# Raw weights' buffers for the last input forms, and an earlier request for u, in a one-core attention, gate and mixer kernel

## The chip, the cores and the metric

The kernel runs on one NeuronCore of a Trainium2 chip, as one launch. The metric is the time of an execution on the device in microseconds, the median of several runs. Before the change it is 718.12 us (three runs, 717.54 to 718.13).

## What is computed

Three stages over `batch = 4`, `seq = 448`, `d_model = 768` (12 heads of 64), all in float32 accuracy. The change lies in the second half of the third one, the channel mixer `u + relu(u @ w_ch1) @ w_ch2`, with `d_ch = 1536`.

```python
def _attn_ref(q, k, v):
    scores = scale * np.matmul(q, k.transpose(0, 1, 3, 2)) - np.log(S)
    attn = 1.0 / (1.0 + np.exp(-scores))
    return np.matmul(attn, v).astype(np.float32)

def _moe_ref(x, w_val, conv_w, w_out):
    for k in range(K):
        gate_pre += conv_w[k][None, None, :] * xp[:, k:k + S, :]
    gate = 1.0 / (1.0 + np.exp(-gate_pre))
    val = x @ w_val
    return (gate * val @ w_out).astype(np.float32)

def _moe2_ref(x, w_tok1, w_tok2, w_ch1, w_ch2):
    xt = x.transpose(0, 2, 1)
    h = np.maximum(xt @ w_tok1, 0.0) @ w_tok2
    u = x + h.transpose(0, 2, 1)
    h2 = np.maximum(u @ w_ch1, 0.0) @ w_ch2
    return (u + h2).astype(np.float32)
```

## The kernel before

Matrix products take each float32 operand as two parts, a high one in the format `F32R` and the rest, and add three matmuls (high by high, low by high, high by low). The first 384 us hold attention, the gated layer and the token mixer; `u` is left in a DRAM scratch, `uscr`, channels by positions. The change touches only what follows.

The channel mixer goes over the 1792 positions in four tiles of 512, 512, 384 and 384 (`TILES`), and over the 1536 inner channels in 12 steps of 128 (`fc`). In the first two tiles step `fc` is a `ch1` (18 matmuls into one of the two PSUM buffers `psh`, then a `split` with relu by ScalarE and VectorE into `r`), followed by the `ch2` of the step before (18 matmuls into six accumulators `pso`). At the last step each of the six accumulators gets the input added: `u` is loaded again into a buffer of the tag `gate` (`ur`, by `u_load`), VectorE adds the accumulator to it (L778), and SP sends it to `out` (L780).

The third and fourth tile share their first matrix product by Strassen's and Winograd's scheme: seven products of half size in place of eight. For it, `sums(i)` forms sums of the weights beside the second tile and stores them through SP into the scratch `fscr`; their operands `sum_s` and `sum_h` take both buffers of the tag `raw` of the pool `rp["a"]`, which held the raw weights before. `turned_load(k)` loads four blocks of `u` for the third and fourth tile (`ub`), and `turned(k)` makes the seven forms of the input of group `k` from them, with two more buffers, `t1` and `t2` (`ut`), for differences; k goes from 0 to 2. A form is a high part by ScalarE (L926) and a low part by VectorE (L930), with differences by VectorE (L934) between them.

After the second tile, `seven(i)` runs six times: seven calls of `product`, each nine matmuls into one of two PSUM buffers `psm`, emptied by ScalarE (L983) or by an add on VectorE (L987) into buffers `um`. Behind every `seven` but the first stand two `ch2` of the third tile; the fourth tile's `ch2` come last. The weights of a product, a form `wf`, are loaded by POOL's queue (`form_load`, L962) into six buffers, and every product asks for the form that is six ahead.

The tag `gate` has six buffers of 2 KB a partition, given out in turn, and `ub`, `ut`, `ur` and `um` all use them. A buffer is given again once its last reader, a DMA too, is through.

From the second tile's second step on the order is written out by hand (`tc.manual_schedule`): each engine and each DMA queue takes its instructions in program order and waits only for semaphores. The table `beside` says behind which `ch1` of the second tile which helper stands: `turned_load(2)` behind the tenth (`fc` 9) and `turned(2)` behind the last (`fc` 11). Behind the last `ch1` also stand six `form_load` and `ur_load`, which asks for all six `ur`:

```python
if fn is ch1 and fc == KF - 1:
    for _ in range(KD):
        form_load()
    ur_load(t)
```

For the first tile nothing of this is written out: there the last `ch2` asks for each `ur` itself, in a part of the program that a scheduler orders, which puts these loads some eleven us ahead of their use.

Of the kernel before, what the change touches and what calls it, by code (L numbers as in the profile page):

```python
# [8 lines left out]
F32 = mybir.dt.float32  # L9
# [25 lines left out]
def tile_kernel(ctx, tc, qT, kT, v, w_val, conv_w, w_out, w_tok1, w_tok2, w_ch1, w_ch2, out):  # L35
# [11 lines left out]
    P = 128  # L47
# [12 lines left out]
    KH = KD // 2  # L60
# [5 lines left out]
    W = max(TILES)  # L66
# [6 lines left out]
    NJ = TILES[-1]  # L73
# [3 lines left out]
    def f(ap):  # L77
        return ap.bitcast(F32)
# [95 lines left out]
    both = tc.alloc_tile_pool(name="both", bufs=1, side="left")  # L174
# [466 lines left out]
    rp = {}  # L641
# [75 lines left out]
        return ops  # L717


    def u_load(t, j, name):  # L720
        u = both.tile([P, W], F32, tag="gate", bufs=6, name=name)
        lo, hi = sum(TILES[:t]), sum(TILES[: t + 1])
        for b in range(lo // S, (hi - 1) // S + 1):
            c0, c1 = max(lo, b * S), min(hi, (b + 1) * S)
            nc.sync.dma_start(u[:, c0 - lo : c1 - lo], uscr[b, j, :, c0 - b * S : c1 - b * S])
        return u[:, : hi - lo]

    def prep_load(t, j):
        us_t[t, j] = u_load(t, j, "u")
# [31 lines left out]
    def ur_load(t):  # L761
        for j in range(KD):
            ur[t, j] = u_load(t, j, "ur")

    def ch2(t, fc):
        n_t = TILES[t]
        r = r_t.pop((t, fc))
        for j in range(KD):
            if fc == 0:
                acc[j] = pso.tile([P, 512], F32, tag=f"o{j}", name="pso")  # L770
            for n, (a, c) in enumerate(((0, 0), (1, 0), (0, 1))):
                nc.tensor.matmul(  # L772
                    acc[j][:, :n_t], wch[fc][1][a][:, j * P : (j + 1) * P], r[c],
                    start=fc == 0 and n == 0, stop=fc == KF - 1 and n == 2,
                )
            if fc == KF - 1:
                u = ur.pop((t, j)) if (t, j) in ur else u_load(t, j, "ur")
                nc.vector.tensor_tensor(out=u, in0=acc[j][:, :n_t], in1=u, op=ALU.add)  # L778
                lo = sum(TILES[:t])
                nc.sync.dma_start(out[j * P : (j + 1) * P, lo : lo + n_t], u)  # L780

    with tc.manual_schedule():
# [23 lines left out]
        for b in range(B):  # L806
            val, outs, after = dense_steps(b, tok[3] if b else ([], []))
            if b:
                early = val[0] + tok[0] + val[1] + tok[1]
                rest = sum(val[2:], []) + tok[2]  # L810
                if b + 1 < B:
                    ops = first.pop(0)
                    n = len(PRE)
# [59 lines left out]
    def form_room():  # L873
        if not room:
            fc = form_room.at
            form_room.at += 1
            if 0 < fc < CHAN_LATE:
                get = w_tile if fc < CHAN_HELD else wo_tile
                room.extend(get().rearrange("p (c m) -> p c m", c=2) for _ in range(2))
            else:  # L880
                t = rp["p" if fc else "a"].tile([P, 2, 2, HALF], F32R, tag=f"wch{fc}_0", bufs=1, name="bf")
                room.extend(t[:, n] for n in range(2))
        return room.pop(0)
# [30 lines left out]
    ub = {}  # L914

    def turned_load(k):
        ub[k] = [u_load(t, k + h, "ub") for h in (0, KH) for t in (2, 3)]

    def turned(k):
        b11, b12, b21, b22 = ub.pop(k)  # L920
        t1, t2 = [both.tile([P, W], F32, tag="gate", bufs=6, name="ut")[:, :NJ] for _ in range(2)]
        to = {}

        def high(name, src):
            to[name] = src, form_room()
            nc.scalar.activation(out=to[name][1][:, 0], in_=src, func=AF.Copy)  # L926

        def low(name):
            src, x = to.pop(name)
            nc.vector.tensor_tensor(out=x[:, 1], in0=src, in1=f(x[:, 0]), op=ALU.subtract)  # L930
            bform[name, k] = x

        def sub(o, x, y):
            nc.vector.tensor_tensor(out=o, in0=x, in1=y, op=ALU.subtract)  # L934

        high("b11", b11)
        sub(t1, b12, b11)
        high("t1", t1)
        low("b11")
        sub(t2, b22, t1)  # L940
        high("t2", t2)
        low("t1")
        high("b22", b22)
        low("t2")
        sub(b12, b22, b12)
        high("t3", b12)
        low("b22")
        high("b21", b21)
        low("t3")
        sub(t1, b21, t2)  # L950
        high("t4", t1)
        low("b21")
        low("t4")
# [4 lines left out]
    def form_load():  # L958
        if queue:
            i, name = queue.pop(0)  # L960
            t = both.tile([P, 2, HALF], F32R, tag="xs", bufs=KD, name="wf")
            nc.gpsimd.dma_start(t, fscr[i, spot[name]])  # L962
            held_f[i, name] = t
# [13 lines left out]
    def seven(i):  # L977
        def spare():
            return both.tile([P, W], F32, tag="gate", bufs=6, name="um")[:, :NJ]

        def out(ps):
            t = spare()
            nc.scalar.activation(out=t, in_=ps, func=AF.Copy)  # L983
            return t

        def add(o, x, y):
            nc.vector.tensor_tensor(out=o, in0=x, in1=y, op=ALU.add)  # L987

        m1 = out(product(i, "a11", "b11"))
        u = spare()  # L990
        add(u, product(i, "s2", "t2"), m1)
        m5 = out(product(i, "s1", "t1"))
        v = spare()
        add(v, u, m5)
        add(v, product(i, "s4", "b22"), v)
        nc.sync.dma_start(rscr[2 * i], v)
        add(u, product(i, "s3", "t3"), u)
        add(m5, u, m5)
        nc.sync.dma_start(rscr[2 * i + 1], m5)
        r = rp["a"].tile([P, 2, 2, NJ], F32R, tag="raw", bufs=2, name="rr")  # L1000
        add(m1, product(i, "a12", "b21"), m1)
        split(r[:, 0, 0], r[:, 0, 1], m1, relu=True)
        add(u, product(i, "a22", "t4"), u)
        split(r[:, 1, 0], r[:, 1, 1], u, relu=True)
        for n in range(2):
            r_t[2, 2 * i + n] = [r[:, n, c] for c in range(2)]
# [3 lines left out]
    def r_load(fc):  # L1010
        if fc < KF:
            back[fc] = both.tile([P, W], F32, tag="gate", bufs=6, name="rl")[:, :NJ]
            nc.sync.dma_start(back[fc], rscr[fc])

    def r_split(fc):
        if fc < KF:
            r = rp["p"].tile([P, 2, W], F32R, tag="r", bufs=2, name="r")
            r = [r[:, c, :NJ] for c in range(2)]
            split(*r, back.pop(fc), relu=True)
            r_t[3, fc] = r  # L1020
# [11 lines left out]
    for fn, t, fc in order[:cut]:  # L1032
# [5 lines left out]
        elif fn is ch2 or t or fc >= EARLY:  # L1038
            fn(t, fc)
    with tc.manual_schedule():  # L1040
        beside = {1: (sums, 0), 2: (sums, 1), 3: (sums, 2), 4: (turned_load, 0, sums, 3), 5: (turned, 0)}
        beside |= {6: (sums, 4), 7: (turned_load, 1, sums, 5), 8: (turned, 1), 9: (turned_load, 2), 11: (turned, 2)}
        for fn, t, fc in order[cut:]:
            fn(t, fc)
            if fn is ch1:
                todo = beside.get(fc, ())
                for n in range(0, len(todo), 2):
                    todo[n](todo[n + 1])
            if fn is ch1 and fc == KF - 1:
                for _ in range(KD):  # L1050
                    form_load()
                ur_load(t)
        for i in range(KF // 2):
            seven(i)
            if i:
                for fc in (2 * i - 2, 2 * i - 1):
                    ch2(2, fc)
        for fc in range(2):
            r_load(fc)
            r_split(fc)  # L1060
        ur_load(2)
        ch2(2, KF - 2)
        ch2(2, KF - 1)
        r_load(2)
        for fc in range(KF):
            r_load(fc + 3)
            if fc == KF - 2:
                ur_load(3)
            ch2(3, fc)
            r_split(fc + 2)  # L1070
# [42 lines left out]
```

## Time and profile before

| | before |
|---|---|
| median of 3 runs | 718.12 us |
| profiled execution | 716.71 us |
| its span, first to last instruction | 714.9 us |
| mean granted clock of TensorE | 0.995 of full |
| TensorE busy | 702.4 us, 98% |
| VectorE / ScalarE / GpSimd busy | 480.8 / 305.3 / 90.5 us |
| moved by DMA | 128.16 MB, 179 GB/s in the mean |

Times in the rows are microseconds from the start of the span. L778 is line 778 of the kernel before. PE is TensorE's matmuls, PEld its weight loads, DVE is VectorE, ACT ScalarE, POOL GpSimd; SPq is SyncE's queue of DMA issues. A row of a timeline merges neighbouring instructions of one kind (x18: eighteen of them) and gives in brackets how long the engine was idle before and what ended that.

### The profile page before, as it was taken

What the parts mean: (1) busy time and instruction counts of PE and PEld (TensorE: products, weight loads), DVE (VectorE), ACT (ScalarE), POOL (GpSimd) and SP (SyncE); (2) the same over time, 40 slices, a digit from 0 to 9 for tenths busy, and PEclk for the clock granted to TensorE, in tenths of its full rate; (3) what the DMA queues carried; (4) which work ended last, traced back from release to release, by engine and by line L of the source; (5) the groups of instructions that cost most, each with busy time, mean ns of one, the idle gap of its engine ahead of it and who ended that gap; (6) DMA issues with size and microseconds to landing.
All of it is one profiled execution on the core that took longest, in us unless ns stands there. A gap on an engine that the chain in (4) does not pass through costs nothing.

```text
span 714.9 us, 11033 instructions
## 1 busy us (share of the span) xinstructions
PE 702.4 (98%) x4210; PEld 576.1 (81%) x4210; DVE 480.8 (67%) x789; ACT 305.3 (43%) x454; POOL 90.5 (13%) x128
## 2 busy tenths in 40 slices
PE   8999999999999999999999999999999699999998
PEld 3444444699999999999988888888888599999997
DVE  1799775479899998976778999557771533232322
ACT  5899888347336435624733444312331211111110
POOL 0000110003213213301340000000000122220000
PEclk9999999999999999999999999999999999999999
DMA  9747998504346324236994555339882986664533
GB/s 296 250 136 235 276 289 271 168 26 99 64 164 178 69 96 131 67 127 188 224 350 146 169 166 177 89 119 340 291 280 62 298 243 182 193 182 131 184 102 110
DMA packets 102212, 128.16 MB, mean 179 GB/s; under 512 B 35072, under 2 KB 89104, under 8 KB 102160
## 3 DMA queue, kind: packets, MB, share of 16 engines
q1 hardware_dynamic: 90672, 90.40, 41.6%
q0 software_dynamic: 11056, 36.61, 15.9%
q8 instruction: 33, 0.54, 0.3%
q10 hardware_dynamic: 432, 0.46, 0.2%
q14 instruction: 19, 0.16, 0.1%
HBM read 83.98 MB, written 37.16 MB: 169 GB/s over the span
## 4 chain that ended last, share of the span: by engine, by line
PE 92%; DMA 3%; DVE 2%; ACT 1%; issue 1%; SPq 0%; DVEq 0%; ACTq 0%
PE psd L359 24%; PE pso L772 23%; PE psh L745 12%; PE psm L970 9%; PE psy L296 8%; PE pss L281 8%; PE pst L423 4%; PE pst L436 4%; DMA raw<-w_ch 1%; DMA out<-ur 1%; DMA k<-kT 1%; DMA ur<-uscr 1%; ACT ga L283 0%; DVE dec_a L135 0%; DVE x2T L440 0%
## 5 line engine op out<-in xcount | busy, mean ns | idle before, releaser
L283 ACT ACTIVATE ga<-pss,bias_s 128x896 f32<-128x896 f32 x84 | 83.5, 1004 | 19.7 <-PE pss L281 19.1
L359 PE MATMUL psd<-gv,wo 128*128 128x448 f32 x432 | 88.0, 362 | 0.0
L359 PE MATMUL psd<-xs,w 128*128 128x448 f32 x432 | 87.7, 362 | 0.0
L359 PEld LDWEIGHTS psd<-xs,w 128*128 128x128 f32 x432 | 80.8, 187 | 6.0 <-issue 0.7
L359 PEld LDWEIGHTS psd<-gv,wo 128*128 128x128 f32 x432 | 81.0, 187 | 5.4
L281 PE MATMUL pss<-q,k 64*64 64x448 f32 x672 | 78.9, 540 | 1.2 <-DMA k<-kT 0.7
L296 PE MATMUL psy<-ga,v 64*64 64x448 f32 x672 | 77.6, 536 | 0.0
L329 DVE SCALAR_TENSOR_TENSOR gate<-xb,cw,gate 128x448 f32<-128x448 f32 x96 | 72.2, 752 | 2.6
L281 PEld LDWEIGHTS pss<-q,k 64*64 64x64 f32 x672 | 26.3, 134 | 39.7 <-issue 29.3
L296 PEld LDWEIGHTS psy<-ga,v 64*64 64x64 f32 x672 | 25.7, 133 | 37.4 <-issue 35.9
L962 POOL DMA_DIRECT2D wf<-fscr x42 | 22.2, 528 | 245.9 <-PE psh L745 167.1
L135 DVE SCALAR_TENSOR_TENSOR dec_a<-raw,dec_a 128x768 int32<-128x768 int32 (+2 forms) x38 | 33.4, 880 | 20.8 <-ACT dec_a L123 20.8
L123 ACT ACTIVATE dec_a<-dec_a,exp_b 128x768 int32<-128x768 int32 (+3 forms) x39 | 33.0, 858 | 32.6 <-DVE dec_a L120 32.6
L987 DVE TENSOR_TENSOR um<-psm,um 128x384 f32<-128x384 f32 x30 | 16.7, 556 | 43.8 <-PE psm L970 43.0
L394 POOL COPY pl<-st 128x1024 uint16<-128x1024 uint16 x21 | 32.1, 1529 | 102.2 <-ACT gate L340 50.8
L970 PE MATMUL psm<-bf,wf 128*128 128x384 f32 x162 | 36.8, 342 | 6.1 <-ACT um L983 6.1
L370 ACT ACTIVATE gv<-gate 128x448 fp32r<-128x448 f32 x24 | 13.9, 578 | 56.5 <-DVE gate L368 56.5
L94 DVE SCALAR_TENSOR_TENSOR r<-psh,r 128x512 fp32r<-128x512 f32 x22 | 15.0, 688 | 30.1 <-ACT r L92 30.1
L772 PE MATMUL pso<-r,wo 128*128 128x512 f32 (+1 forms) x162 | 35.0, 371 | 0.0
L970 PEld LDWEIGHTS psm<-bf,wf 128*128 128x128 f32 x162 | 29.5, 193 | 6.5 <-ACT um L983 6.4
L772 PEld LDWEIGHTS pso<-r,wo 128*128 128x128 f32 x162 | 29.7, 188 | 4.2
L772 PE MATMUL pso<-r,w 128*128 128x512 f32 (+1 forms) x144 | 30.7, 368 | 0.0
(200 smaller groups left out, 1270.7 us busy)
## 6 DMA issues: line engine op xcount, KB each, us to landing
raw<-w_ch SPq DMA_DIRECT2D x24, 768.0 KB, 4.4
wf<-fscr POOLq DMA_DIRECT2D x42, 384.0 KB, 4.4
v<-v SPq DMA_DIRECT2D x24, 224.0 KB, 6.4
uscr<-x2T POOLq DMA_DIRECT2D x24, 224.0 KB, 2.4
q<-qT SPq DMA_DIRECT2D x23, 224.0 KB, 4.5
k<-kT SPq DMA_DIRECT2D x22, 224.0 KB, 4.7
raw<-w_out POOLq DMA_DIRECT2D x6, 768.0 KB, 8.5
fscr<-sum_h SPq DMA_DIRECT2D x6, 768.0 KB, 3.4
```

The source lines that it names most:

```text
L123: nc.scalar.activation(out=t["a"], in_=t["a"], func=AF.Relu, scale=8.0, bias=exp_b)
L135: nc.vector.scalar_tensor_tensor(out=t["a"], in0=hi, scalar=-0x80000000, in1=t["a"], op0=ALU.bitwise_and, op1=ALU.bitwise_or)
L281: nc.tensor.matmul(ps[cols, j, :S], k[rows, keys], q[rows], start=True, stop=True)
L283: nc.scalar.activation(out=a, in_=ps[:, :, :S], func=AF.Sigmoid, bias=bias_s, scale=QK_SCALE)
L296: nc.tensor.matmul(y_t[i + h][cols, :S], v_t[i][rows, c, cols], a[rows, j], start=c == 0, stop=c == NB - 1)
L329: nc.vector.scalar_tensor_tensor(out=acc, in0=x[:, t : t + S], scalar=w, in1=acc, op0=ALU.mult, op1=ALU.add)
L359: nc.tensor.matmul(ps[:, :S], w(a, kk), s[:, c, :], start=kk == 0 and n == 0, stop=kk == KD - 1 and n == 2,)
L394: nc.gpsimd.tensor_copy(back.rearrange("p (n h) -> p h n", h=2), st.rearrange("p h c d -> p h (c d)"))
L423: nc.tensor.matmul(ps[:, :HALF], a, x[:, m], start=n == 0, stop=n == len(mm) - 1)
L745: nc.tensor.matmul(ps[:, :n_t], wch[fc][0][a][:, kk * P : (kk + 1) * P], us_t[t, kk][:, c, :], start=kk == 0 and n == 0, stop=kk == KD - 1 ...
L772: nc.tensor.matmul(acc[j][:, :n_t], wch[fc][1][a][:, j * P : (j + 1) * P], r[c], start=fc == 0 and n == 0, stop=fc == KF - 1 and n == 2,)
L970: nc.tensor.matmul(ps, w[:, a, k * P : (k + 1) * P], bform[x, k][:, c], start=k == 0 and n == 0, stop=k == KH - 1 and n == 2,)
```

## The change

`u_load` may be given a place instead of taking a `gate` buffer. For the last group, k = 2, `turned_load` takes both `raw` buffers of `rp["a"]`: the four `ub` go into the first, and `t1` and `t2` into the second, so that this group uses no `gate` buffer. And `ur_load(t)` moves from behind the last `ch1` of the second tile to behind its tenth (`fc` 9), right behind `turned_load(2)`.

```diff
-    def u_load(t, j, name):
-        u = both.tile([P, W], F32, tag="gate", bufs=6, name=name)
+    def u_load(t, j, name, u=None):
+        u = both.tile([P, W], F32, tag="gate", bufs=6, name=name) if u is None else u
...
     def turned_load(k):
-        ub[k] = [u_load(t, k + h, "ub") for h in (0, KH) for t in (2, 3)]
+        at = [None] * 6
+        if k == KH - 1:
+            spare = [rp["a"].tile([P, 4, NJ], F32, tag="raw", bufs=2, name="ub") for _ in range(2)]
+            at = [spare[n // 4][:, n % 4] for n in range(6)]
+        ub[k] = [u_load(t, k + h, "ub", at[2 * n + t - 2]) for n, h in enumerate((0, KH)) for t in (2, 3)], at[4:]
 
     def turned(k):
-        b11, b12, b21, b22 = ub.pop(k)
-        t1, t2 = [both.tile([P, W], F32, tag="gate", bufs=6, name="ut")[:, :NJ] for _ in range(2)]
+        (b11, b12, b21, b22), t = ub.pop(k)
+        if t[0] is None:
+            t = [both.tile([P, W], F32, tag="gate", bufs=6, name="ut")[:, :NJ] for _ in range(2)]
+        t1, t2 = t
...
             if fn is ch1 and fc == KF - 1:
                 for _ in range(KD):
                     form_load()
+            if fn is ch1 and fc == 9:
                 ur_load(t)
```

On no engine does the change move an instruction past another: TensorE's and POOL's rows are the same, and on SP, VectorE and ScalarE the same operations stand in the same order, with other waits. (Line numbers of the kernel after are up to 7 higher.) In the rows below, a semaphore DMAHW0 to DMAHW7 is one of those that SP's DMAs count up in turn; DVE, PE and Activation are the engines' own.

SP's queue, from the loads of `ub` for k = 2 to the first loads of `ur` for the second tile, before:

```order
L912 DMA fscr<-sum_s 128x4x384 [waits DMAHW7_49,DVE_49]
L725 DMA ub<-uscr 128x320 [waits DMAHW0_49,DVE_49]
L725 DMA ub<-uscr 128x64 [waits DMAHW1_49,DMASW4_49]
L725 DMA ub<-uscr 128x384 [waits DMAHW2_49,DVE_49]
L725 DMA ub<-uscr 128x320 [waits DMAHW3_49,DVE_49]
L725 DMA ub<-uscr 128x64 [waits DMAHW4_49,DMASW7_49]
L725 DMA ub<-uscr 128x384 [waits DMAHW5_49,DVE_49]
L725 DMA ur<-uscr 128x384 [waits DMAHW1_49,DMAHW6_49,DMAHW0_49,DVE_49]
L725 DMA ur<-uscr 128x128 [waits DMAHW7_49]
```

and after:

```order
L912 DMA fscr<-sum_s 128x4x384 [waits DMAHW7_49,DVE_49]
L725 DMA ub<-uscr 128x320 [waits DMAHW6_49,DMAHW0_49]
L725 DMA ub<-uscr 128x64 [waits DMAHW1_49,DMASW4_49]
L725 DMA ub<-uscr 128x384 [waits DMAHW2_49]
L725 DMA ub<-uscr 128x320 [waits DMAHW3_49]
L725 DMA ub<-uscr 128x64 [waits DMAHW4_49,DMASW7_49]
L725 DMA ub<-uscr 128x384 [waits DMAHW5_49]
L725 DMA ur<-uscr 128x384 [waits DVE_49]
L725 DMA ur<-uscr 128x128 [waits DMAHW7_49]
```

The loads of `ub` no longer wait for VectorE but for a store of SP (DMAHW6, that of `sum_h`); the first `ur` no longer waits for DMAs, only for VectorE, whose count here is one of `turned(1)`.

ScalarE at the end of `turned(2)`, where the first two evictions of a product (`um`) stand, before:

```order
L926 ACTIVATE bf<-ub 128x384 [waits DMAHW5_49]
L926 ACTIVATE bf<-ub 128x384 [waits DVE_49]
L926 ACTIVATE bf<-ub 128x384 [waits DMAHW4_49,DMAHW3_49]
L926 ACTIVATE bf<-ut 128x384 [waits DMAHW2_49,DVE_49]
L983 ACTIVATE um<-psm 128x384 [waits DMAHW2_49,DMAHW6_49,DVE_49,DMAHW7_49,PE_49,Activation_49]
L983 ACTIVATE um<-psm 128x384 [waits DMAHW3_49,DVE_49,DMAHW4_49,PE_49,Activation_49]
```

and after:

```order
L932 ACTIVATE bf<-ub 128x384 [waits DMAHW5_49]
L932 ACTIVATE bf<-ub 128x384 [waits DVE_49]
L932 ACTIVATE bf<-ub 128x384 [waits DMAHW4_49,DMAHW3_49]
L932 ACTIVATE bf<-ub 128x384 [waits DMAHW2_49,DVE_49]
L989 ACTIVATE um<-psm 128x384 [waits DMAHW6_49,DMAHW2_49,DMAHW7_49,DVE_49,PE_49]
L989 ACTIVATE um<-psm 128x384 [waits DMAHW3_49,DMAHW4_49,DVE_49,PE_49]
```

Nothing moved; `t1` and `t2` are now called `ub`, and the evictions still wait for SP's DMAs, the store of the `ur` whose `gate` buffer they take among them (DMAHW2 for the first, DMAHW4 for the second).

## Rows read from the trace of the kernel before

**Rows 1.** The page: busy us of each engine, share of the span, instructions.

```profile
PE 702.4 (98%) x4210; PEld 576.1 (81%) x4210; DVE 480.8 (67%) x789; ACT 305.3 (43%) x454; POOL 90.5 (13%) x128
```

**Rows 2.** The chain of waits, 540 to 600: start us, us, what.

```profile
557.83 5.04 DMA ur<-uscr
...
565.50 6.25 DMA out<-ur
...
571.99 0.50 ACT um L983
```

**Rows 3.** TensorE's timeline, 526 to 618: start us, us, engine, line, operation.

```profile
563.14 0.69 PE L970 MATMUL psm<-bf,wf 128*128 128x384 f32 x3
...
572.53 1.33 PE L970 MATMUL psm<-bf,wf 128*128 128x384 f32 x3 [6.09 <-ACT um L983]
...
592.72 3.28 PE L772 MATMUL pso<-rr,wch__3250 128*128 128x384 f32 x18
...
598.96 0.68 PE L970 MATMUL psm<-bf,wf 128*128 128x384 f32 x3
...
609.88 6.40 PE L772 MATMUL pso<-rr,w 128*128 128x384 f32 x36
```

**Rows 4.** Stretches: length, each engine's busy us, granted clock, DMA share, GB/s.

```profile
572.50:575.50 3.00, 2.96 (x9) 2.97 (x10) 0.56 (x1) 0.00 (x0) 0.00 (x0) 0.51 0.53 196
575.50:592.70 17.20, 17.20 (x100) 17.20 (x100) 7.91 (x15) 3.06 (x6) 5.81 (x11) 1.00 0.88 244
592.70:714.90 122.20, 118.74 (x686) 118.42 (x684) 33.94 (x63) 14.76 (x29) 12.14 (x23) 1.00 0.50 153
```

**Rows 5.** SP's queue of DMA issues, end of the first and the second tile.

```profile
455.25 5.81 SPq L725 DMA_DIRECT2D ur<-uscr  x12
467.37 3.32 SPq L780 DMA_DIRECT2D out<-ur  x6
...
531.61 0.53 SPq L912 DMA_DIRECT2D fscr<-sum_s  x1
533.32 4.50 SPq L725 DMA_DIRECT2D ub<-uscr  x6
557.46 7.94 SPq L725 DMA_DIRECT2D ur<-uscr  x12
565.50 6.62 SPq L780 DMA_DIRECT2D out<-ur  x6
```

**Rows 6.** VectorE's timeline at the same two places.

```profile
466.66 3.67 DVE L778 TENSOR_TENSOR ur<-pso,ur 128x512 f32<-128x512 f32 x6
...
537.59 0.56 DVE L930 TENSOR_TENSOR wo<-ut,wo 128x384 fp32r<-128x384 f32 x1
...
561.73 0.56 DVE L930 TENSOR_TENSOR bf<-ut,bf 128x384 fp32r<-128x384 f32 x1
562.99 2.10 DVE L778 TENSOR_TENSOR ur<-pso,ur 128x512 f32<-128x512 f32 x3 [0.70 <-DMA ur<-uscr]
```

**Rows 7.** Median us from issue to landing: first tile's first store; `sum_s` of 531.61.

```profile
out<-ur SPq DMA_DIRECT2D x1, 256.0 KB, 2.0
...
fscr<-sum_s SPq DMA_DIRECT2D x1, 768.0 KB, 6.7
```

**Rows 8.** POOL's queue of DMA issues, 526 to 600.

```profile
552.04 1.89 POOL L962 DMA_DIRECT2D wf<-fscr  x3 [167.10 <-PE psh L745]
...
566.75 0.53 POOL L962 DMA_DIRECT2D wf<-fscr  x1 [1.04 <-DMA ur<-uscr]
```

**Rows 9.** Form loads' us to landing: issued 555 to 556, and all of 545 to 600.

```profile
DMA to landing us min/median/max: 5.3/5.5/5.6
...
DMA to landing us min/median/max: 3.1/4.6/8.2
```

**Rows 10.** Two more stretches, columns as in rows 4.

```profile
470.00:472.00 2.00, 2.00 (x10) 1.67 (x9) 0.32 (x1) 0.00 (x0) 0.00 (x0) 1.00 1.05 396
...
563.10:566.30 3.20, 3.20 (x19) 2.99 (x18) 2.47 (x4) 0.00 (x0) 0.53 (x1) 1.00 0.81 231
```

## The prediction

> **What bounds the kernel now.** I read the page's busy times first: TensorE is busy for 702.4 of 714.9 us [rows 1], so only what makes TensorE idle, or slows it, can move the time. Then the chain of waits, to find a stretch that isn't TensorE. Around the end of the second tile (its last `ch2`, then the first two calls of `seven`) it leaves TensorE for a load of `ur`, a store of `ur` to `out` and an eviction on ScalarE, and only then comes the next product [rows 2]. Third, TensorE in order of time: it starts the first product at 563.14, runs two products at full pace, and is then idle for 6.09 us until 572.53 [rows 3]. It has two PSUM buffers for products; the third product needs the first one's, which ScalarE must empty into a buffer of the tag `gate`, and that buffer still holds the first `ur`, on its way to `out`.
>
> The same stretch also runs slowly behind the gap. The granted clock is 0.51 from 572.5 to 575.5 and 1.00 from 575.5 on [rows 4]: the lower of the two levels (1.2 and 2.4 GHz) after an idle stretch, then the upper.
>
> The loss is the stretch against the same work undisturbed. Fourteen products run from 563.14 to 592.72, which is 29.58 us. A later call of `seven`, seven products, runs from 598.96 to 609.88, 10.92 us or 1.56 a product [rows 3]; two calls are 21.84. So 29.58 - 21.84 = 7.74 us are lost. In parts: two products at full pace end at 563.14 + 3.12 = 566.26, and the third starts at 572.53, 6.27 later; the third's nine matmuls fill 572.5 to 575.5 [rows 4], 3.00 us for 1.56, so 1.44 more; the other eleven run at full pace, within 0.03. From 592.7 on TensorE is busy without a pause at full clock until the tail [rows 4], so what is saved here moves everything behind it.
>
> Why the store is late: SP's queue issues the twelve loads of `ur` only from 557.46 to 565.40, and the six stores stand behind them [rows 5]. Before that it issues nothing from 537.8 on, since it waits for VectorE's `turned(2)`, whose operands fill all six `gate` buffers. The first add is through by 563.7 [rows 6], but its store is issued at 565.50 and lands 6.25 us later, with the last loads of `ur` and the form loads moving beside it [rows 2].
>
> **The change, part by part.**
>
> *The last input forms in the raw buffers.* No computation is added: VectorE and ScalarE get the same operations of the same shapes in the same order, so `turned(2)` still ends on VectorE at 561.73 + 0.56 = 562.29 [rows 6]. What is new is what the six loads of `ub` wait for: no longer the `gate` operands of `turned(1)`, but the raw buffers' last stores, `sum_h` and `sum_s` of `sums(5)`. The later was issued at 531.61 [rows 5] and landed 6.7 us later [rows 7], at 538.3. SP stands still for them, and behind them stand only the loads of `ur`, until the outputs. If all six wait for 538.3 and take the 4.50 us of issue that they took before [rows 5], they are issued by 542.8; `turned(2)` wants them at 556. Cost: nothing, under some 13 us of cover, less the landing. The raw buffers are wanted again by `rr` in the first `seven`, some ten us after `turned(2)` is through; also nothing.
>
> *The `ur` loads behind the tenth step.* SP's order doesn't change: `ub`, then `ur`, then `out`. Only the waits do. The `gate` buffers are now free once `turned(1)` has ended (537.59 + 0.56 = 538.15 [rows 6]), so the twelve loads follow `ub` at once: 542.8 + 5.81 (the first tile's twelve [rows 5]) = 548.6, and even at the 6.25 us of this tile's store [rows 2] they are there by 555. Neither SP's queue nor POOL's issues anything in that stretch before [rows 5, 8], so it collides with nothing, and the form loads, from 552 on, lose the `ur` traffic beside them. The adds need `ur` at 562.3; some 7 us are left over.
>
> *What is late next* is the store of the first `ur`. VectorE goes from `turned(2)` to the adds at 562.29. The first tile is the model, since its `ur` is loaded early: six adds in 3.67 us from 466.66, the first store issued at 467.37, 0.71 after the first add began [rows 5, 6]. So the first store is issued at 562.29 + 0.71 = 563.0. How long it takes is not shown for this place; the bounds are 2.0 us (the first tile's first store [rows 7]) and 6.25 (this tile's, behind the `ur` loads [rows 2]). I take 2.0: as in the first tile nothing is queued ahead, since the first six form loads are issued by 556 and the last of them took at most 5.6 us even with `ur` beside them [rows 9]. Then it lands at 565.0, as the first product ends (563.14 + 1.56, and the last matmul's tail); ScalarE's 0.50 us [rows 2] make 565.5; and the third product's buffer is free before the second product ends at 566.26. The margin is 0.7 us: each us of landing over 2.7 costs one.
>
> The next in line is VectorE: its six adds end at 562.29 + 3.67 = 565.96, and the add that empties the second product's buffer (0.56, as its other operations on 128x384) ends at about 567.1, against 567.8 when the third product ends. The second to fourth stores, issued some 0.6 us apart, land by 568; the buffers that they free are wanted at 566.5, 567.9 and 568.5. No stall above half a us; I take none.
>
> The sum: 7.74 us off a profiled execution of 716.71 (span 714.9) is 708.97. That execution was 1.41 below the median of 718.12, so against the median it is 718.12 - 7.74 = **710.4 us**.
>
> *The form loads behind the stores.* The gap gave the DMA a rest that now goes: 1.57 MB of stores (six of 256 KB) meet one form load of 0.39 MB per 1.56 us. The seventh and eighth form load are issued as the first two products end (about 565.2, and 566.75 [rows 8]) and wanted at 572.5 and 574.1, when the seventh and eighth product start. Form loads land in 4.6 us in the median and 8.2 at most [rows 9]. At 8.2 the eighth would come at 574.95, 0.9 late. DMA moved 396 GB/s for the first tile's stores, and 231 in the mixed stretch from 563.1 [rows 10]. From 564 to 567, 2.35 MB of stores and form loads come up. At 396, 1.16 MB are left, 2.9 us of work, and with the 2.0 us of a lone store as latency the eighth lands at 572: in time. At 231 it is 1.66 MB, 7.2 us, and the eighth is some 2 us late; all that the fourteenth product needs (stores, eight form loads, 0.6 MB of `rscr`, 5.3 MB) is there at 587 instead of 583.4, near 4 late. I take the upper rate, because in the slower stretch the loads of `ur` in their short rows and SP's issue held it down, and keep the lower one for the range.
>
> A rule of the Trainium skill speaks against this: "DMA: Bandwidth & Descriptors", section "Specifications", gives some 358 GB/s as the limit of one core's share of HBM. All that is issued in the 21.84 us (six stores, fourteen form loads, four `rscr` stores, 7.86 MB) is 360 GB/s, just over that; by it I estimate 21.96 us for the stretch and 710.5 for the kernel. The trace's 396 GB/s in a stretch of writes to HBM [rows 10] stands above the page's figure already.
>
> **The rivals.**
> - *The first store stays slow.* If form loads get in first and it lands after 4 to 6.25 us, the third product waits 1.3 to 3.55 us; with another 1.44 if the clock falls again, 711.7 to 715.4. Against it: the first tile's 2.0.
> - *Form loads late.* The gap closes, but the eighth to fourteenth form load comes 1 to 4 us late, as worked out above: 711.4 to 714.4.
> - *The change doesn't do what it says.* If SP's queue were still held until `turned(2)`, by a raw buffer say, the loads of `ur` would come as now: 718.1. Against it: what now stands first in SP's order waits for stores that landed by 538.3.
> - *Slower.* The mechanism is the clock: late form loads make repeated pauses, and the clock stays at its lower level for all twelve products behind the second. Each costs 1.44 us more, 17.3 in all, less 7.74: 727.7. It decides from 5.4 slow products on. Against it: at 3.0 us a product the form loads are wanted at half the rate, so DMA catches up; and in the trace one slow product was enough to return to full clock [rows 4].
>
> **How the numbers follow.** Full gain 0.70 (710.4), slow first store 0.12, late form loads 0.12, no effect 0.03, slower 0.03. The range must leave out at most 2 in 10: from 708.9 (the 1.41 by which single executions differ, taken off) to 713.8, which takes in most of both partial cases. A difference of 0.2% (1.4 us) is about what can be told from no change; faster by more than that is 0.70 + 0.12 + 0.12 = 0.94, within it 0.03, slower 0.03.
>
> **What the changed profile would show.** Right: loads of `ur` issued between 538 and 549 on SP; the first store issued at about 563.0 and landing in 2 to 3 us; no idle TensorE behind 566, granted clock 1.00 there, 21.8 us from the first product to the first `ch2` of the third tile; a span of about 707.2; no `ur` in this part of the chain of waits. Wrong: an idle stretch ahead of the third product that ends on ScalarE and a store (first rival), one ahead of the eighth or a later product that ends on a form load (second), or loads of `ur` at 557 (third). I would also be wrong if `turned(2)` took longer on the raw buffers, which no row here prices: each us there moves the adds by one, with 0.7 to spare.

## The result, and the profile after

| | before | after |
|---|---|---|
| median (runs of one chip) | 718.01 us (717.54 to 718.13, 4 runs) | 710.10 us (709.44 to 710.43, 4 runs) |
| profiled execution, its span | 716.71 us, 714.9 us | 710.43 us, 708.7 us |
| first product to first `ch2` of the third tile | 29.58 us | 22.48 us |
| mean granted clock of TensorE | 0.995 | 1.00 |

After takes 0.989 of the time of before (95%: 0.9873 to 0.9907). Forecast were 710.4 us and a gain of 7.74; between the medians lie 7.91.

The queue of SP after, to be held against [rows 5] (start us, us, issues; L725 loads `u`, L780 stores the output):

```profile
531.65 0.53 SPq L912 DMA_DIRECT2D fscr<-sum_s  x1
536.39 2.71 SPq L725 DMA_DIRECT2D ub<-uscr  x6
539.14 5.65 SPq L725 DMA_DIRECT2D ur<-uscr  x12
563.25 3.44 SPq L780 DMA_DIRECT2D out<-ur  x6
```

The loads of `ur`, which began at 557.46, now begin at 539.14 and are all issued by 544.8. The first store was issued at 565.50 and is now at 563.25. The six stores take 3.44 us of issue instead of 6.62, since their adds no longer wait for loads.

VectorE after, to be held against [rows 6]: the end of `turned(2)`, the six adds, and the first add that empties a product's PSUM buffer.

```profile
561.39 1.23 DVE L936 TENSOR_TENSOR bf<-ub,bf 128x384 fp32r<-128x384 f32 x2
562.54 3.67 DVE L778 TENSOR_TENSOR ur<-pso,ur 128x512 f32<-128x512 f32 x6
567.15 0.56 DVE L993 TENSOR_TENSOR um<-psm,um 128x384 f32<-128x384 f32 x1 [0.94 <-ACT um L989]
```

The six adds follow at once and run without a pause; before, the first of them waited 0.70 us for a load and the row stopped after three. `turned(2)` ends at 561.39 + 1.23 = 562.62. Its operations on the raw buffers are as long as on the old ones.

The chain of waits after, at the place of [rows 2]:

```profile
563.25 3.15 DMA out<-ur
...
566.56 0.50 ACT um L989
...
567.10 19.01 PE psm L976 x108
```

The loads of `ur` have left the chain. The store has not: it takes 3.15 us instead of 6.25, and ScalarE's eviction and the third product still hang on it. What that costs is on TensorE's timeline, as in [rows 3]:

```profile
563.47 0.68 PE L976 MATMUL psm<-bf,wf 128*128 128x384 f32 x3
...
567.10 0.79 PE L976 MATMUL psm<-bf,wf 128*128 128x384 f32 x3 [0.32 <-ACT um L989]
...
585.95 3.28 PE L772 MATMUL pso<-rr,wch__3250 128*128 128x384 f32 x18
```

The third product waits 0.32 us, where it waited 6.09. The stretch is 585.95 - 563.47 = 22.48 us, against 21.84 for undisturbed work: 7.10 of the 7.74 us are gone. Stretches of this time (columns as in [rows 4]):

```profile
567.10:568.80 1.70, 1.70 (x10) 1.70 (x11) 0.56 (x1) 0.00 (x0) 0.51 (x1) 1.00 0.76 120
568.80:585.90 17.10, 17.10 (x100) 17.10 (x100) 7.82 (x15) 3.05 (x6) 5.81 (x11) 1.00 1.04 313
```

The granted clock is 1.00 behind the pause, and TensorE is busy in all of the 17.10 us, so no form load is late in this execution. Of the page, the row of [rows 1]:

```profile
PE 701.8 (99%) x4210; PEld 574.3 (81%) x4210; DVE 481.0 (68%) x789; ACT 305.4 (43%) x454; POOL 88.9 (13%) x128
```

In this execution the first product starts 0.33 us later than in that of before, and the tail is 0.6 longer, so the span is shorter by 6.2 us, not by 7.1. A second profiled execution has 21.97 us for the stretch and a span of 708.0.

### The profile page after: what moved, and what is told of

Its sections match the earlier page's. It is cut to its first block, busy times and chain, and to the rows that moved or that the text cites. A ratio compares the mean times of both kernels' runs of the same rounds, so it can differ in the third digit from the quotient of the medians.

```text
span 708.7 us, 11027 instructions
## 1 busy us (share of the span) xinstructions
PE 701.8 (99%) x4210; PEld 574.3 (81%) x4210; DVE 481.0 (68%) x789; ACT 305.4 (43%) x454; POOL 88.9 (13%) x128
## 4 chain that ended last, share of the span: by engine, by line
PE 93%; DVE 3%; DMA 2%; ACT 1%; issue 1%; SPq 0%; DVEq 0%; ACTq 0%
PE psd L359 24%; PE pso L772 23%; PE psh L745 12%; PE psm L976 9%; PE pss L281 9%; PE psy L296 8%; PE pst L423 4%; PE pst L436 4%; DMA raw<-w_ch 1%; ACT ga L283 1%; DMA k<-kT 0%; DMA out<-ur 0%; DVE dec_a L135 0%; DVE x2T L440 0%; DVE ub L940 0%
## 5 line engine op out<-in xcount | busy, mean ns | idle before, releaser
L329 DVE SCALAR_TENSOR_TENSOR gate<-xb,cw,gate 128x448 f32<-128x448 f32 x96 | 75.0, 781 | 2.6
L92 ACT ACTIVATE r<-psh 128x512 fp32r<-128x512 f32 x22 | 12.9, 591 | 40.9 <-PE psh L745 40.9
```

Source lines behind the costliest of these rows:

```text
L329: nc.vector.scalar_tensor_tensor(out=acc, in0=x[:, t : t + S], scalar=w, in1=acc, op0=ALU.mult, op1=ALU.add)
```

## The experiments

The theory: the loads of `ur` came late because they waited for `turned(2)`; they made the store late, and ScalarE's first `um` waited for the store's buffer. Rivals: the gain is the buffer's alone, the moved request's alone, or the traffic's; and form loads, now without the rest that the gap gave them, are near to being late. Times are medians, with the ratio to the kernel before on the same chip.

**The raw buffers alone.** The request for `ur` goes back to its old place, behind the last `ch1`.

```diff
             if fn is ch1 and fc == KF - 1:
                 for _ in range(KD):
                     form_load()
-            if fn is ch1 and fc == 9:
                 ur_load(t)
```

> The raw buffers alone: the request for ur stays behind the last ch1. Theory (the buffers do all of it, since SP's queue runs ahead of the program and keeps the order ub, ur, out either way): as the changed kernel, about 710.1 us, loads of ur issued at 539 to 545, 22.5 us from the first product to the first ch2 of the third tile. Rival (the earlier place of the request matters): loads of ur later than 545, up to 718 us. It also serves as a second look at the changed kernel for the runs beside it.

709.92 us, ratio 0.9885 (0.9861 to 0.9908). It comes out as the same program as the changed kernel, instruction for instruction and wait for wait. SP's row of `ur` and TensorE's timeline:

```profile
540.24 5.65 SPq L725 DMA_DIRECT2D ur<-uscr  x12
```

```profile
563.67 0.68 PE L976 MATMUL psm<-bf,wf 128*128 128x384 f32 x3
...
566.29 1.31 PE L976 MATMUL psm<-bf,wf 128*128 128x384 f32 x6
...
585.67 3.28 PE L772 MATMUL pso<-rr,wch__3250 128*128 128x384 f32 x18
```

The loads are early although the program asks for them sixteen us later, behind the last `ch1`: on SP nothing stands between that place and the new one, so SP comes to them as soon as their buffers are free. The move of `ur_load` does nothing; the raw buffers bring the whole gain. The move alone was not tried: `t1` and `t2` would have to take `gate` buffers whose `ur` are added on VectorE behind `turned(2)`, so `turned(2)` would wait for itself.

**Free buffers for the first `um`, in the kernel before.** The first four `um` go into a raw buffer, which is idle there, and the loads of `ur` stay late.

```diff
     def seven(i):
+        four = rp["a"].tile([P, 4, NJ], F32, tag="raw", bufs=2, name="um4") if i == 0 else None
+        left = [four[:, n] for n in range(4)] if i == 0 else []
+
         def spare():
+            if left:
+                return left.pop(0)
             return both.tile([P, W], F32, tag="gate", bufs=6, name="um")[:, :NJ]
```

> The kernel before, in which only the first seven's four um come from a raw buffer, free since the sums: the first eviction no longer waits for a store of ur, while ur is still loaded late. Theory (the late loads hold VectorE too, whose add for the second product stands behind the six adds of ur, the last of which ran at 571.1 to 571.8): the idle stretch moves from the third to the fourth product and shrinks from 6.1 to some 4.5 us (567.8 to 572.4), the clock still falls; 716.4 us. Rival (the waiting buffer was all): no idle TensorE, 710.3 us.

716.72 us, ratio 0.9981 (0.9964 to 0.9998). Chain of waits, then VectorE, then TensorE of this kernel:

```profile
566.15 5.57 DMA ur<-uscr
...
572.80 0.56 DVE um L992
```

```profile
565.11 3.43 DVE L778 TENSOR_TENSOR ur<-pso,ur 128x512 f32<-128x512 f32 x5 [2.06 <-DMA ur<-uscr]
572.19 0.69 DVE L778 TENSOR_TENSOR ur<-pso,ur 128x512 f32<-128x512 f32 x1 [3.66 <-DMA ur<-uscr]
```

```profile
573.40 1.33 PE L970 MATMUL psm<-w,wf 128*128 128x384 f32 x3 [4.64 <-DVE um L992]
```

The wait for the store is gone and the third product runs on, but the fourth stops for 4.64 us: its PSUM buffer is emptied by an add on VectorE, which stands behind six adds, and the last of these waits for a late load of `ur` until 572.19. Two waits stood behind the late loads, nearly equally late; to free the buffer opens only the first. That excludes the buffer alone as the cause, and what both waits have in common are the late loads. The stretch is 29.51 us here, 0.07 less than before; that explains next to nothing of the 1.3 us between the medians, and the profiled execution (717.95) is among the slowest of ten.

**The same buffers in the changed kernel** (the same edit).

> The changed kernel, with the first seven's four um from a raw buffer: the first eviction waits for no store. Theory (the 0.47 us left of the gap, and 0.17 of slower matmuls around it, are the landing of the first store, 3.15 us against the 2.0 forecast): no idle TensorE there, 21.84 us for the fourteen products, 0.6 us less than the changed kernel, 709.5. Rival (what is left comes from VectorE or from form loads): as the changed kernel, 710.1, with idle ahead of another product.

709.98 us, ratio 0.9888 (0.9864 to 0.9912). With the store out of the way the stretch is 563.38 to 585.24, 21.86 us, without a pause. Beside the 22.00 of the raw buffers alone that is 0.14 us, which the times (709.98 and 709.92) can't show. What the changed kernel still loses to the store is 0.1 to 0.6 us, by the execution.

**The first store made late.** In the changed kernel, the second tile's last store goes ahead of its first, so all stores wait for the sixth add.

```diff
+    late = []
...
-                nc.sync.dma_start(out[j * P : (j + 1) * P, lo : lo + n_t], u)
+                late.append((out[j * P : (j + 1) * P, lo : lo + n_t], u))
+                if t != 1 or j == KD - 1:
+                    for d, s in (late[-1:] + late[:-1] if t == 1 else late):
+                        nc.sync.dma_start(d, s)
+                    late.clear()
```

> The changed kernel, with the second tile's last store put ahead of the other five on SP's queue, so that all six wait for the last of the six adds: the first buffer's store is issued at about 566.8 and not at 563.3. Theory (each us by which that store lands later than the end of the second product costs one): landing at 569.5 to 570 (2.7 to 3.2 us as seen), third product at 570.2 to 570.7, 3.4 to 3.9 us idle; 713.5 us, or 714.9 if the clock falls as it did behind the gap of 6.1 us. Rival (the store isn't what the third product waits for): 710 us.

715.75 us, ratio 0.9978 (0.9965 to 0.9992); some 6.6 us above the changed program on the same chip (709.10 and 709.17, below). Chain of waits, then TensorE:

```profile
565.86 3.72 DMA out<-ur
...
569.69 0.50 ACT um L995
```

```profile
570.23 1.33 PE L982 MATMUL psm<-bf,wf 128*128 128x384 f32 x3 [3.83 <-ACT um L995]
...
575.19 0.69 PE L982 MATMUL psm<-bf,wf 128*128 128x384 f32 x3
```

The first store is issued 2.77 us behind the start of the first product, where it was 0.22 ahead of it; it takes 0.57 longer (3.72, not 3.15), and the pause grows by 3.5, from 0.32 to 3.83. Then the clock is down: the five groups of three matmuls from 570.23 to 575.19 take 4.96 us for 2.60. So 3.99 us of pause (from 566.24, where the second product is through) and 2.36 of clock, and the stretch is 28.22 us. Some six of the seven us hang on when the first store is issued. They are not owed to the traffic of the `ur` loads, which are early here too (issued from 539.58). The loss is larger than I expected, by the clock.

**Fewer form loads ahead.** One fewer behind the last `ch1`, then two.

```diff
-                for _ in range(KD):
+                for _ in range(KD - 1):
                     form_load()
```

> The changed kernel, with five form loads ahead in place of six: each form load then has 5.95 us from its issue to its product (four products of 1.56 us, less 0.29 until the issue) and not 7.5. Landing behind the six stores was 5.1 to 5.5 us for the seventh and 5.2 to 7.2 for the eighth. Theory (with six ahead the form loads have over a us to spare): 0 to 1.3 us slower than the changed kernel, 710.0 to 711.3, what idle there is in the first two sevens alone. Rival (form loads are already at their limit behind the stores): pauses of a us and more ahead of several products, 713 or more.

> The same with four form loads ahead: 4.4 us from issue to product, below nearly all landings seen behind the stores (4.4 to 7.2) and about the median of the later ones (4.6). Theory: pauses of half a us to 2 us ahead of most products of the first two sevens, few later; 713 to 718 us, and where pauses repeat the granted clock may fall. This is the slower rival of the prediction brought about on purpose: if short pauses keep the clock at its lower level, the two sevens take over 30 us and the kernel is at 718 or above; if not, it stays below.

709.10 us (ratio 0.9889, 0.9871 to 0.9906) and 709.17 (0.9888, 0.9869 to 0.9907). Neither did what I meant. POOL's issues in the second:

```profile
552.18 1.89 POOL L968 DMA_DIRECT2D wf<-fscr  x3 [167.13 <-PE psh L745]
554.22 0.53 POOL L968 DMA_DIRECT2D wf<-fscr  x1 [0.15 <-issue]
554.90 0.53 POOL L968 DMA_DIRECT2D wf<-fscr  x1 [0.15 <-issue]
555.58 0.53 POOL L968 DMA_DIRECT2D wf<-fscr  x1 [0.15 <-issue]
```

Six loads are issued as before: each product asks for one more, POOL's queue comes to these requests long before the product runs, and six buffers are free. Then I left a buffer or two out in another way, with tiles that are allocated and not used, and asked for five or four loads ahead (of the first of the two; the other has 4 for 5):

```diff
+            if len(given) % 5 == 0:
+                for _ in range(KD - 5):
+                    both.tile([P, 2, HALF], F32R, tag="xs", bufs=KD, name="unused")
```

> The changed kernel with five buffers for form loads in place of six (every sixth one is given out and left unused), so that a form load waits for the product five before its own: about 5.95 us from issue to product, not 7.5. (The run with five requests ahead kept six buffers, and POOL's queue filled them all the same: it was the changed kernel once more.) Theory (form loads, 5.1 to 5.8 us behind the stores in most executions and 7.2 once, have a us and more to spare with six): 0 to 1.3 us above the changed kernel, in the first two sevens alone. Rival (they are at their limit): 3 us and more.

> The same with four buffers: 4.4 us from issue to product, against landings of 4 to 5.5 us with six buffers. Theory: pauses ahead of many products of the first two sevens, 0.5 to 1.5 us each until the stores are through, and a few later: 3 to 9 us above the changed kernel. If short pauses bring the clock down, as the prediction's slower rival says, the granted clock falls and the loss is 15 us or more; if not, it stays at 1.00.

709.88 us (0.9901, 0.9878 to 0.9923) and 709.61 (0.9896, 0.9882 to 0.9911). A tile that nothing reads or writes holds no buffer back, and these are the same program again. None of the four tests the form loads; they are repeats of the changed kernel, and are used as such below.

**Four form buffers.** Two buffers are held by a write of one column ahead of the form loads and one behind all products.

```diff
             if fn is ch1 and fc == KF - 1:
-                for _ in range(KD):
+                held = [both.tile([P, 2, HALF], F32R, tag="xs", bufs=KD, name="held") for _ in range(2)]
+                for w in held:
+                    nc.gpsimd.memset(f(w[:, 0, :1]), 0.0)
+                for _ in range(KD - 2):
                     form_load()
...
+        for w in held:
+            nc.gpsimd.memset(f(w[:, 0, :1]), 0.0)
```

> The changed kernel with four buffers for form loads in place of six: the other two are held by a one-column write ahead of the form loads and another behind the last, so that every form load waits for the product four before its own, 4.4 us from issue to product (in the two earlier tries the unused buffers were taken again, and the program was the changed kernel's). Landings behind the stores are 5.1 to 5.5 us for the seventh and eighth load and 4 to 5 later. Theory (late form loads are short pauses that settle, as with six buffers there is a us or two to spare): a pause of about a us ahead of two to four products in a row behind the stores, up to half a us ahead of others, granted clock at 1.00 or near; 2 to 6 us above the changed kernel, 711 to 716. The prediction's slower rival (repeated short pauses keep the clock at its lower level): granted clock near 0.5 over the first two sevens, 17 us and more above the changed kernel, 726 or more.

712.48 us, ratio 0.9918 (0.9901 to 0.9934), 1 to 2 us above the changed kernel by the ratios (none ran beside it on that chip). TensorE's two pauses, and the stretch around the first:

```profile
570.85 0.77 PE L976 MATMUL psm<-w,wf 128*128 128x384 f32 x3 [0.70 <-DMA wf<-fscr]
...
577.97 0.76 PE L976 MATMUL psm<-w,wf 128*128 128x384 f32 x3 [0.61 <-DMA wf<-fscr]
```

```profile
569.00:575.00 6.00, 5.30 (x31) 4.99 (x30) 2.79 (x5) 0.19 (x2) 1.93 (x4) 1.00 1.10 312
```

Now form loads are late, but by 0.7 us and twice; the stretch takes 24.00 us, and the later `seven` 10.96 to 11.23 instead of 10.92. The granted clock stays at 1.00 through both pauses. So six buffers are enough and four are not quite.

**`turned(2)` a step earlier**, beside the eleventh `ch1` instead of the last.

```diff
-        ..., 9: (turned_load, 2), 11: (turned, 2)}
+        ..., 9: (turned_load, 2), 10: (turned, 2)}
```

> The changed kernel, with turned(2) one step earlier, behind the eleventh ch1, so that VectorE is free when the accumulators of the second tile are done. Theory (the first store is late by turned(2), which ended at 562.5 while the first accumulator was done at 560.1): first store issued at about 560.8 and landed by 564.0, before the first product ends; no idle TensorE, 709.5 us. Rival: ub, loaded at 536 to 542, or turned(2) beside other work delays a ch1 or ch2: 710.5 or more.

709.31 us, ratio 0.9877 (0.9853 to 0.9902); again, beside a repeat of the changed kernel, 709.29 (0.9887, 0.9871 to 0.9904) against 710.42 (0.9905, 0.9890 to 0.9919). VectorE and SP of the first profiled execution:

```profile
559.67 4.09 DVE L778 TENSOR_TENSOR ur<-pso,ur 128x512 f32<-128x512 f32 x6 [3.38 <-PE pso L772]
```

```profile
560.39 3.73 SPq L780 DMA_DIRECT2D out<-ur  x6
```

The adds no longer follow `turned(2)` but TensorE's accumulators. The first store is issued 2.5 us ahead of the first product (562.87 - 560.39) instead of 0.2; though it takes 3.8 us to land (2.2 in the second), no product waits, and the stretches are 21.86 and 21.87 us. The first median lies 0.6 us below the one of the raw buffers alone on its chip. On the chip of the second the changed program has three medians (710.42, and 709.88 and 709.61 of the kernels with untouched tiles), 0.3 to 1.1 us above it. The stretch explains 0.1 to 0.6. It is the best version that was run, by a difference of the size of that among medians of one program (0.8 us).

## Why the prediction was right

**The cause and the sum.** The 7.74 us were put down to the store behind the late loads and to the clock behind the gap. 7.10 us went in the profiled execution. The same program in six more executions (the repeat, the raw buffers alone and the four kernels that came out as this program) needs 21.97 to 22.27 us, so 7.3 to 7.6 went there. The part that is left is the store's. That the median came within 0.3 us of the forecast is in part luck: executions of the kernel before differ by 0.6 us on one chip and by 3.6 on another, and the 7.91 between the medians is more than any of these stretches gives.

**The first store's landing: the mis-sized term.** I took 2.0 us from the first tile, and the margin sentence had the point at 2.7 from which it costs one for one. It took 3.15 us in the profile: by that sentence 0.45 too much, and the third product started at 567.10 instead of 566.63 (two products behind 563.47 + 0.04): 0.47. In the other six executions it took 2.67 to 2.96, and the stretch had 21.97 to 22.27 us, so in the seven the stretch grows with the landing one for one, as the margin sentence has it. So the first rival happened in small, and the first store stands on the path, not beside it. That the first tile was the wrong model is shown by its own rows: its first store took 1.99 or 2.00 us in all fourteen profiled executions, and the second tile's never less than 2.2 (what differs is told at the end). The Trainium skill, "DMA: Bandwidth & Descriptors", section "Anatomy of one DMA — SWDGE (gpsimd) path", gives 2.0 us and the bytes at 436 GB/s for another kind of queue; for 256 KB I estimate 2.6 us from it, which is nearer to these rows than the first tile's 2.0 was, and below all of them.

**The two edits.** I gave the raw buffers the early `ub` and the moved request the early `ur`. That SP's order stays was in the text, and it should have told me that the move is no cause: what it moves in the program it moves past nothing on SP. The raw buffers alone show it. SP's times were as forecast or earlier: `ub` by 542.8 (539.1; the loads began at 536.39 and not at 538.3, since they wait for the store of `sum_h` alone, which landed at 536.3), `ur` between 538 and 549 (539.1 to 544.8), first store at 563.0 (563.25).

**VectorE as the next in line.** No stall was forecast, and none came. In the kernel before it had been one: with the store's wait opened there, VectorE's adds held the fourth product until 573.40. Both waits go with one cause, which is why the sum over the whole gap held; by the store alone it wouldn't have.

**The form loads.** They were forecast in time, and were, but with less to spare than I worked out. The eighth form load after:

```profile
L968 POOL DMA_DIRECT2D wf<-fscr x1: 528/528/528, 567.1 to 567.1; - x1
...
DMA to landing us min/median/max: 7.2/7.2/7.2
```

It landed at 574.3, not at 572, and the eighth product starts at 575.03, 7.93 us behind the third: 0.7 us to spare. In the other six executions of the program it landed in 5.2 to 5.4 us. One premise was off: the first six were to have landed by 561.6, but the last of them, issued at 555.8, took 7.6 us, to 563.4, and the first store was issued ahead of that. And the demand of 7.86 MB in the stretch was too much: 22 us of it at 290 GB/s are 6.4 MB; I put the rest down to loads that are asked for in the stretch and land behind it.

```profile
563.00:585.00 22.00, 21.68 (x124) 21.26 (x123) 11.35 (x21) 3.02 (x6) 6.49 (x13) 1.00 0.95 290
```

So the stretch never asked for the 358 GB/s of the Trainium skill, "DMA: Bandwidth & Descriptors", "Specifications", and it can't say whether that is a limit here; 1.7 us of the kernel with the late store moved 404 GB/s (below).

**The other rivals.** "Doesn't do what it says" is out by SP's rows. "Slower" by pauses that keep the clock low is out where it was nearest: two pauses of 0.6 to 0.7 us in the kernel with four form buffers left it at 1.00. With the store made late, one pause of 4 us took 6.6 us of the 7.7 back, so the first rival's price, 3.55 + 1.44 at most, was too low in its clock. That one slow product was enough to return to full clock held in the kernel before alone: behind the pauses of the late store and of the free `um` buffers five and six groups of three matmuls ran slowly, where a product has three.

## What to carry to other kernels

Where a queue waits only for buffers, the place of a request in the program means little: find what holds its buffers, and give the last user of them others. Before you cost a wait as removed, look for a second one behind the same late transfer, here VectorE's adds in their order behind the store's buffer. And where the next work's first buffer comes back only through a store, count that store's landing with its scatter, 2.0 to 3.8 us here, or move what stands ahead of it.

## What the runs showed of the hardware

**A shorter pause cost more clock.** Three kernels have one long pause of TensorE ahead of a product. First the kernel with the late store, then the kernel before with free `um` buffers, then the kernel before (columns as in [rows 4]):

```profile
567.50:568.50 1.00, 0.00 (x0) 0.00 (x0) 0.00 (x0) 0.00 (x0) 0.00 (x0) 0.92 1.06 365
568.50:570.20 1.70, 0.00 (x0) 0.00 (x0) 0.00 (x0) 0.49 (x1) 0.00 (x0) 0.50 1.10 404
...
574.00:575.00 1.00, 1.00 (x5) 1.00 (x4) 0.56 (x1) 0.01 (x1) 0.30 (x1) 0.50 0.03 12
575.00:576.00 1.00, 1.00 (x7) 1.00 (x6) 0.09 (x1) 0.00 (x0) 0.00 (x0) 0.92 1.00 246
```

```profile
571.00:573.40 2.40, 0.00 (x0) 0.00 (x0) 1.16 (x2) 0.00 (x0) 0.00 (x0) 0.82 1.04 338
...
576.00:579.00 3.00, 3.00 (x11) 3.00 (x10) 0.56 (x1) 0.00 (x0) 0.53 (x1) 0.50 0.47 92
579.00:580.00 1.00, 1.00 (x6) 1.00 (x6) 0.44 (x1) 0.00 (x0) 0.18 (x1) 0.81 0.91 310
```

```profile
568.00:569.00 1.00, 0.00 (x0) 0.00 (x0) 0.21 (x1) 0.00 (x0) 0.00 (x0) 0.82 0.85 289
```

The lower level lasts until about 575.2, 579.4 and 575.5, which is 4.9, 6.0 and 2.9 us behind the restart (570.23, 573.40, 572.53), after pauses of 4.0, 4.8 and 6.3 us. What was lost to it is 2.36, 2.81 and 1.44 us. The clock fell at about 568.3, 572.5 and 568.6 (a mean of 0.92 over 567.5 to 568.5 is 0.84 us at 1.00 and the rest at 0.50), so in the first two TensorE restarted sooner after the fall than in the third (1.9, 0.9 and 3.9 us), and the upper level did not come back the sooner for it: more work ran at half rate. The size of this loss can't be read from the length of the pause.

**The landing of one store scatters in one place and not in another.** The first store of the second tile, 256 KB, took 3.15 us and 2.7 to 3.0 in the same program, 3.8 and 2.2 in two executions of the kernel with `turned(2)` earlier, and 3.72 with the store made late, where the first tile's took 2.0 [rows 7]. In the executions with 3.15 and 3.8 the last of the first six form loads landed only behind the store's issue (563.4 and 563.5); in the second profiled execution of the changed kernel (2.7) and in that of the version with `turned(2)` earlier (2.2) it landed at 562.7, the one ahead of the store's issue at 563.37, the other behind it at 561.14. So this isn't the whole reason.

The traces show a second thing beside it: a DMA that the profile lists as `q14 instruction`, 8 KB. In the seven executions of the changed program, and with the first `um` in a raw buffer or four form buffers, it starts about 0.1 us behind the store's first packet. It takes 0.58 us where the store lands in 2.67 (two executions), 0.74 where it lands in 2.96 and 0.84 where it lands in 3.15, and these nine stand in nearly one order by either time (two neighbours change places). In the first tile a DMA of the same kind and size starts with the store's issue and is through ahead of its first packet, 0.84 us later, and the store takes 2.0 in all fourteen executions. In the executions with 3.8, 3.72 and 2.2 it is not there; form loads moved 0.12, 0.39 and under 0.01 MB between the store's issue and its landing, and another DMA of instructions (`q8`, 16 KB) ended 0.5 us behind the store's first packet in the one with 3.8 and ahead of it in the one with 2.2. No run moved these DMAs alone, so they go with the late landing and are not shown to be its cause.
